# Four tiles of 320 tokens become tiles of 320, 448 and 512 in the first layer of an attention and two-layer feed-forward kernel

## The chip, the cores and the metric

The kernel runs on one core of one Trainium2 chip. The metric is device time in microseconds (us) of one execution, as the median of several runs. Beside it stands one profiled execution, from which all rows below come. Engines are named as in the profile: PE (TensorE matmuls), PEld (its weight loads), DVE (VectorE), ACT (ScalarE), POOL (GpSimd), SP (SyncE, which issues the transfers).

## The reference

Windowed attention with a linear distance bias, then two feed-forward layers, on 4 sequences of 576 tokens, 8 heads of 64:

```python
scores = scale * np.matmul(q, k.transpose(0, 1, 3, 2))
bias = slopes[:, None, None] * (-np.abs(rel).astype(np.float32))[None, :, :]
mask = (rel >= 0) & (rel < window)                   # window = 128
attn = softmax(np.where(mask, scores + bias[None], -1e9))
x = np.matmul(attn, v)                               # 2304 tokens x 512
h = x @ w_in;  x = (h * np.clip(h + 3.0, 0.0, 6.0) / 6.0) @ w_out      # layer 1, 512 -> 2048 -> 512
r = np.maximum(x @ w_in2, 0.0);  out = (s * r * r + b) @ w_out2        # layer 2, same sizes
```

Everything is float32.

## The kernel before, in words

**Layer 1.** A matrix product in float32 is made of three products of parts: each operand is split into a rounded high part and the rest. The 2304 tokens go through layer 1 in tiles. A tile takes 16 steps `f`, one for each 128 of the 2048 inner columns. Step `h` is 12 matmuls (4 blocks of 128 inputs, three products of parts) into one bank of PSUM; then ACT (`relu`) and DVE (`product`) make the gated value, ACT (`hi`) and DVE (`lo`) split it; step `o` is 12 matmuls into four banks that stay for the tile. Every matmul has 128x128 weights, and as many columns as the tile has tokens. Tiles 0 and 1 (256 tokens each) share their matmuls from step 4 on, 512 columns wide. Tiles 2 and 3 have 256 tokens; their `o` step covers two products with one matmul and takes 8. Tiles 4 to 7 have 320 tokens, the last 320 of each of the four sequences. `end` scales the four banks and stores them to `x2d` in DRAM.

**Attention.** A `Unit` is one head of one group of tokens, and units go in pairs of heads, 16 pairs for the four groups of 320. On PE a pair of that kind makes: scores `q` (line 606 here, 8 matmuls on quarters of the array, 64x64), one score matmul `hs` for the last half block (line 626), transposes `t` of the softmax weights (line 703: two for one head and three for the other) and the values product `v` (line 747, 8 matmuls on halves of the array, 128x64). Between them DVE takes row minima, ACT exponentials, POOL the division and the masks. Scores, transposes and values each take one of three banks (`tag="a", bufs=3`). The tokens of tile `t` have their attention while tile `t - 1` runs.

**Weights of layer 2.** Layer 2 uses sums and differences of blocks of its weights. A `Pair` loads 1 MB of the raw weights (two transfers, `load`), rebuilds floats from the given words (`high`, `rest` on ACT, `shift`, `sign` on DVE, `add` on POOL), forms differences (`sums`, DVE), splits them (`hi` on ACT, `lo` on DVE and POOL) and stores them to DRAM (`wh`, `wo`), from where layer 2 streams them. There are 16 pairs, all made during layer 1. They load into two buffers by turns and compute in a third (`work`).

**Order.** The program is a table written out by hand: each operation has a slot and a rank in it, `at(slot, rank, fn)`, and a table `MOVED` shifts single ones. Each engine works its list strictly in this order. A step `h` stands every second slot; step `o(f)` stands two steps after `h(f)`, so that PE alternates `o` and `h`. Attention pieces stand in the gap behind an `h`. While any tile but the last runs, `h` has a single bank (`tag="h"`), so `h(f + 1)` waits until `product(f)` has read it.

```python
starts = [74 + LATER, 97] + [first + 10 * i for i in range(2 * NP - EARLY)]     # slots at which pairs begin
self.raw = rawbuf[self.i % 2 if self.i >= EARLY else 0]                         # Pair.load
self.work = work() if self.i >= EARLY else rawbuf[1].bitcast(F32)
```

## Time and profile before

| | |
|---|---|
| median of 3 runs | 870.03 us (869.93 to 870.09) |
| profiled execution | 869.65 us, its span 867.9 us |
| PE busy | 860.3 us (99%), 5735 instructions |
| DVE, ACT, POOL busy | 615.7 (71%), 515.9 (59%), 347.9 us (40%) |
| transfers | 183.07 MB, mean 211 GB/s |

The span runs from the first to the last instruction; the profiled execution's time has 1.75 us more around it. Since matmuls are pipelined, the time of a matmul is read from the start of one row to the start of the next, not from its duration.

### The profile page before, as it was taken

How to read it: one execution, taken by the hardware profiler on the slowest of the kernel's cores; microseconds unless marked ns; L12 is line 12 of the kernel's file. 1: busy time of each engine (PE TensorE's matmuls, PEld its weight loads, DVE VectorE, ACT ScalarE, POOL GpSimd, SP SyncE). 2: the span in 40 equal slices, each digit the busy share in tenths (PEclk: the TensorE clock that was granted, in tenths of full speed). 3: DMA queues.
4: the chain of work that ended last, by engine and by line, in shares of the span. 5: the costliest groups of instructions: out<-in, count | busy, mean ns of one | idle time of the engine just before them, and what ended most of it. 6: DMA issues, size and time to landing. Idle time of an engine off the chain costs nothing.

```text
span 867.9 us, 16152 instructions
## 1 busy us (share of the span) xinstructions
PE 860.3 (99%) x5735; PEld 791.1 (91%) x5737; DVE 615.7 (71%) x1368; ACT 515.9 (59%) x1165; POOL 347.9 (40%) x549
## 2 busy tenths in 40 slices
PE   8999999999999999999999999999999999999998
PEld 5997778898989999999999999998899988999887
DVE  6869984577877666767656536779857789577784
ACT  7868985566666555656545436665256655366551
POOL 5647651345554544454444303462114450144200
PEclk9999999999999999999999999999999999999999
DMA  9526443536566555556463628787888887777873
GB/s 330 181 69 193 153 147 107 174 119 215 188 206 212 171 169 193 180 182 227 143 202 121 255 79 297 257 318 243 268 281 294 291 278 256 261 254 266 296 244 114
DMA packets 66879, 183.07 MB, mean 211 GB/s; under 512 B 9968, under 2 KB 29680, under 8 KB 58352
## 3 DMA queue, kind: packets, MB, share of 16 engines
q1 hardware_dynamic: 66800, 182.06, 62.3%
q8 instruction: 45, 0.74, 0.4%
q14 instruction: 34, 0.28, 0.1%
HBM read 143.13 MB, written 38.80 MB: 210 GB/s over the span
## 4 chain that ended last, share of the span: by engine, by line
PE 96%; ACT 1%; DVE 1%; issue 1%; DMA 1%; POOL 0%; SPq 0%; ACTq 0%
PE h L1004 23%; PE o L1052 23%; PE h L1547 20%; PE o L1481 20%; PE v L747 2%; PE s L606 1%; PE t L869 1%; PE tv L884 1%; PE t L703 1%; PE s L838 1%; PE s L591 1%; PE v L948 1%; PE s L626 1%; ACT P L860 0%; DMA raw<-qkv0p 0%
## 5 line engine op out<-in xcount | busy, mean ns | idle before, releaser
L1052 PE MATMUL o<-g,w 128*128 128x320 f32 (+2 forms) x1264 | 228.4, 328 | 0.2 <-DVE g L1029 0.2
L1052 PEld LDWEIGHTS o<-g,w 128*128 128x128 f32 x1264 | 192.3, 188 | 16.8 <-issue 6.2
L1004 PE MATMUL h<-both,w 128*128 128x320 f32 (+2 forms) x1200 | 197.7, 313 | 0.4 <-DVE t L1018 0.4
L1004 PEld LDWEIGHTS h<-both,w 128*128 128x128 f32 x1200 | 178.5, 188 | 7.7 <-DVE t L1018 0.9
L1018 DVE SCALAR_TENSOR_TENSOR t<-t,h 128x320 f32<-128x320 f32 (+2 forms) x116 | 56.0, 483 | 104.2 <-ACT t L1015 104.1
L1015 ACT ACTIVATE t<-h 128x320 f32<-128x320 f32 (+2 forms) x116 | 50.4, 435 | 130.6 <-PE h L1004 130.3
L1547 PE MATMUL h<-x,wstream 128*128 128x384 f32 x612 | 115.4, 335 | 0.0
L1547 PEld LDWEIGHTS h<-x,wstream 128*128 128x128 f32 x612 | 106.4, 188 | 0.8 <-ACT s L1557 0.6
L1481 PE MATMUL o<-wstream,i 128*128 128x512 f32 (+1 forms) x588 | 104.2, 333 | 0.0
L1481 PEld LDWEIGHTS o<-wstream,i 128*128 128x128 f32 x588 | 89.1, 188 | 11.3
L1581 ACT ACTIVATE g<-g,scalar 128x384 f32<-128x384 f32 x96 | 58.6, 610 | 39.4 <-DVE g L1566 37.0
L1481 PE MATMUL o<-both,i 128*128 128x256 f32 (+1 forms) x444 | 78.2, 332 | 0.0
L1547 PE MATMUL h<-x,both 128*128 128x384 f32 x396 | 76.4, 334 | 0.0
L1481 PEld LDWEIGHTS o<-both,i 128*128 128x128 f32 x444 | 66.6, 188 | 8.6
L1025 ACT ACTIVATE g<-t 128x320 fp32r<-128x320 f32 (+2 forms) x116 | 54.1, 466 | 28.4 <-DVE t L1018 27.8
L1029 DVE TENSOR_TENSOR g<-t,g 128x320 fp32r<-128x320 f32 (+2 forms) x116 | 61.9, 534 | 12.6 <-ACT g L1025 11.0
L1604 POOL TENSOR_TENSOR g<-g 128x384 f32<-128x384 f32 x24 | 24.3, 1014 | 112.4 <-PE h L1547 95.8
L1547 PEld LDWEIGHTS h<-x,both 128*128 128x128 f32 x396 | 69.3, 188 | 0.0
L1565 DVE TENSOR_TENSOR g<-h,s 128x384 f32<-128x384 f32 x72 | 39.8, 553 | 31.2 <-PE h L1547 22.5
L732 POOL TENSOR_SCALAR_AFFINE_SELECT W<-F 128x128 f32<-128x128 f32 (+1 forms) x128 | 38.0, 334 | 43.2 <-ACT F L707 41.2
L1221 POOL TENSOR_TENSOR work<-raw 128x512 int32<-128x512 int32 x28 | 29.9, 1086 | 50.3 <-DVE raw L1212 12.5
L1331 DVE SCALAR_TENSOR_TENSOR i<-g,scalar,i 128x768 fp32r<-128x768 f32 x48 | 49.2, 1072 | 0.6 <-ACT i L1330 0.6
(161 smaller groups left out, 1391.2 us busy)
## 6 DMA issues: line engine op xcount, KB each, us to landing
raw<-w SPq DMA_DIRECT2D x53, 512.0 KB, 5.5
wstream<-wo SPq DMA_DIRECT2D x24, 1024.0 KB, 4.9
both<-wo SPq DMA_DIRECT2D x18, 1024.0 KB, 5.9
wstream<-wh SPq DMA_DIRECT2D x18, 768.0 KB, 6.0
wstream<-wh SPq DMA_DIRECT2D x12, 1024.0 KB, 5.7
both<-wh SPq DMA_DIRECT2D x12, 1024.0 KB, 5.2
wh<-raw SPq DMA_DIRECT2D x16, 512.0 KB, 3.0
wo<-raw SPq DMA_DIRECT2D x16, 512.0 KB, 3.2
```

The costliest lines, as they stand in the source:

```text
L732: nc.gpsimd.affine_select(out=u.W[:, o : o + r], in_=self.F[:, q : q + r], fill=0.0, base=k - 1, compare_op=ALU.is_ge, pattern=[[s, r]], c ...
L1004: nc.tensor.matmul(self.ps, lhsT=w[:, wp, cc * P : (cc + 1) * P], rhs=self.values(cc, xp), start=m == 0, stop=m == 3 * CC - 1,)
L1015: nc.scalar.activation(self.a, self.ps, AF.Relu, bias=3.0)
L1018: nc.vector.scalar_tensor_tensor(out=self.a, in0=self.a, scalar=6.0, in1=self.ps, op0=ALU.min, op1=ALU.mult)
L1025: nc.scalar.activation(self.g[:, 0], self.a, AF.Copy)
L1029: nc.vector.tensor_tensor(out=self.g[:, 1], in0=self.a, in1=hi, op=ALU.subtract)
L1052: nc.tensor.matmul(self.sums()[d][:, : n * self.n], lhsT=w[:, wp, DM + d * P : DM + (d + 1) * P], rhs=self.g[:, gp : gp + n], start=f == 0 ...
L1331: nc.vector.scalar_tensor_tensor(out=out[:, :, 1], in0=src, scalar=b, in1=hi.bitcast(F32), op0=ALU.add, op1=ALU.subtract,)
L1481: nc.tensor.matmul(self.acc[k][c][:, out], lhsT=g[:, gp, c * P : (c + 1) * P], rhs=w[:, cols], start=k in (0, 1, 5) and p == 0 and i == 0, ...
L1547: nc.tensor.matmul(self.ps[first], lhsT=w[:, wp, cc], rhs=x[:, cc, xp], start=n == first and m == 0, stop=m == 5, skip_group_check=True,)
L1565: nc.vector.tensor_tensor(out=g, in0=self.ps[n], in1=self.s[j], op=ALU.add)
L1581: nc.scalar.activation(g, g, AF.Copy, scale=s_sb)
```

## The change

The last 1280 tokens are cut into five groups instead of four: the third sequence's last 320 tokens become groups of 128 and 192. Three tiles replace four: 320, 320 + 128 and 192 + 320 tokens. The units of the last four groups are of a new class, `LateUnit`, whose pairs begin every 4 slots, where pairs began every 8, and which goes from scores to values in 10 slots, where it was 16. The inputs `x` of all tiles lie in one stretch `both`; those of the 512-wide tiles begin 8 numbers (32 bytes) later in it than the others. A `Pair` now has two buffers in all: one for the raw weights, into which the high parts are written, and one for the sums, in which the rests are left in place; high and low parts are stored by a transfer each. Its stages take 9 slots in the first seven pairs and 4 in the others; the pairs begin at other slots, the last five in the last tile with a fresh raw buffer for each of the last four. `end` takes the four banks one by one. The table `MOVED` gets entries for the new class and some others.

```diff
-    groups = [(b, qa, qb) for qa, qb in ((0, 2), (2, NB)) for b in range(B)]
+    groups = [(b, 0, 2) for b in range(B)]
+    groups += [(0, 2, NB), (1, 2, NB), (2, 2, 3), (2, 3, NB), (3, 2, NB)]
+    TILES = ((0,), (1,), (2,), (3,), (4,), (5, 6), (7, 8))
...
+    XPLACES = (0, 0, 22, 0, 20, 0, 14)
+    both = xpool.tile([P, 30 * N1A + 16], F32R, name="both")
+    AHEAD = 8
...
+            x = both[:, XPLACES[t] * N1A + (AHEAD if t < 2 or n == 512 else 0) :][:, : 2 * CC * n]
...
+    class LateUnit(Unit):
+        def plan(self, s):
...
+                at(s + 1, 20.5, self.scores)
...
+                    at(s + 2, 20.7, self.half_scores)
...
+            at(s + 2, 32 + odd / 2, self.minima)
+            at(s + 3, 33 + odd / 2, self.exps)
+            at(s + 5 + odd, 31, self.weights)
+            k = s + odd
+            at(k + 7, 20, self.transposes)
...
+                at(s + 11, 20, self.values)
...
         def plan(self, s, load):
             self.s = s
+            k = lambda i: s + ((0, 0, 1, 2, 4, 4, 6, 7, 7, 8), (0, 0, 0, 1, 1, 2, 2, 2, 3, 3))[s >= NARROW][i]
...
         def load(self):
-            self.raw = rawbuf[self.i % 2 if self.i >= EARLY else 0]
-            self.work = work() if self.i >= EARLY else rawbuf[1].bitcast(F32)
+            i = self.i - FRESH
+            if i < 0:
+                self.raw = rawbuf[0]
+            else:
+                self.raw = wtile(i, [P, 4 * DM], I32, f"raw_{self.i}")
+            self.work = rawbuf[1 if i < 0 else i % 2].bitcast(F32)
...
-            nc.sync.dma_start(out=dst, in_=out)
+            nc.sync.dma_start(out=dst[:, :, :HB], in_=hi)
+            nc.sync.dma_start(out=dst[:, :, HB:], in_=lo)
...
-    starts = [74 + LATER, 97] + [first + 10 * i for i in range(2 * NP - EARLY)]
+    NARROW = hslot[5, 0]
+    starts = [80, 96, 110, 124, 138, 152, 165]
+    starts += [NARROW + 4 + 7 * i for i in range(4)] + [last + i for i in (1, 7, 12, 17, 22)]
+    FRESH = 12
...
-            Pair(i, i % NP, i // NP).plan(s, s - 5)
+            Pair(i, i % NP, i // NP).plan(s, s - (4 if s < NARROW else 3))
...
+            if u.g < 5:
+                u.plan(hslot[u.g, 0] - 20 - 4 * (H - 1 - u.h))
+            else:
+                t, i = (5, 2 * (u.h // 2) + (u.g == 5)) if u.g < 7 else (6, 2 * (u.h // 2) + (u.g == 8))
+                u.plan(hslot[t, 0] - 46 + 4 * i)
```

**On PE, in the first tile of 320** (step 4 of it). In the names, `v_2_3` are the values of heads 2 and 3, `s_2_6` the scores of head 6, `P` the softmax weights, `W` their masked transposes, the last number a buffer's. Before, the values product `v` of one pair of heads (the last two of its eight rows are shown) and the scores `q` of a later pair stand in one gap, directly behind each other, ahead of step `o`.

```order
L747 MATMUL v_2_3_3586<-W_2_2_3472,rv_2_2_3215 64x64
L747 MATMUL v_2_3_3586<-W_2_3_3525,rv_2_2_3215 64x64
L606 MATMUL s_2_6_3595<-raw_2_6_3340 64x192
L606 MATMUL s_2_7_3596<-raw_2_6_3340 64x192
L606 MATMUL s_2_6_3595<-raw_2_6_3340 64x192
L606 MATMUL s_2_7_3596<-raw_2_6_3340 64x192
L606 MATMUL s_2_6_3595<-raw_2_6_3340 64x192
L606 MATMUL s_2_7_3596<-raw_2_6_3340 64x192
L606 MATMUL s_2_6_3595<-raw_2_6_3340 64x192
L606 MATMUL s_2_7_3596<-raw_2_6_3340 64x192
L1052 MATMUL o_0_3436<-g_3_3566,w_3_633 128x320
```

In the new program the same tile has, in the gap behind step 3, three transposes and the scores of a pair:

```order
L1129 MATMUL h_3_3583<-both,w_3_634 128x320 x12
L796 MATMUL t_2_3_3596<-ident,P_2_3_3393 128x128 x2
L796 MATMUL t_2_3_3596<-ident,P_2_2_3388 128x128
L698 MATMUL s_2_4_3612<-raw_2_4_3398 64x192
L698 MATMUL s_2_5_3613<-raw_2_4_3398 64x192
L698 MATMUL s_2_4_3612<-raw_2_4_3398 64x192
L698 MATMUL s_2_5_3613<-raw_2_4_3398 64x192
L698 MATMUL s_2_4_3612<-raw_2_4_3398 64x192
L698 MATMUL s_2_5_3613<-raw_2_4_3398 64x192
L698 MATMUL s_2_4_3612<-raw_2_4_3398 64x192
L698 MATMUL s_2_5_3613<-raw_2_4_3398 64x192
L1177 MATMUL o_0_3513<-g_1_3543,w_1_366 128x320
```

The values of the pair before it stand a gap later, behind `h` of step 4, with `hs` ahead of them and a transpose behind them. So what stood in one gap is now in two. From the second tile of 256 on, before has 18 stretches of matmuls on parts of the array in such gaps (14 of `v` with `q` of this kind, 2 of the earlier kind of `v` with `q`, 2 of `v` alone); the new program has 38 (4 with both, 16 of `q` alone, 18 of `v` alone). Of the 18, 13 are followed by a transpose or by `hs`, which take the whole array. Between `h0_13` and `h0_14` in the shared part of tiles 0 and 1, two stretches that stood apart now stand together.

**On SP**, in the second tile of 320 of the old program and in the tile of 448 of the new one. Before, the load of a pair's raw weights goes to the buffer that the pair two earlier used, and the stores come from three buffers.

```order
L1191 DMA raw_202<-w 128x1024 x2
L568 DMA rv_2_4_4353<-v 128x512
L1282 DMA wo<-raw_201 128x2x512 x2
L1282 DMA wo<-staging_early 128x2x512
L1282 DMA wo<-work 128x512
```

Now all transfers of two pairs that follow each other use the same two buffers (202 raw, 203 sums), and the load stands directly behind the stores:

```order
L1398 DMA wo<-raw_202 128x2x256
L1399 DMA wo<-raw_203 128x2x256
L1398 DMA wo<-raw_202 128x2x256
L1399 DMA wo<-raw_203 128x2x256
L1398 DMA wo<-raw_203 128x256
L1399 DMA wo<-raw_203 128x256
L1398 DMA wo<-raw_202 128x2x256
L1399 DMA wo<-raw_203 128x2x256
L1313 DMA raw_202<-w 128x1024 x2
L660 DMA rv_3_6_5168<-v 128x2x192
```

A load that went out ahead of the stores of the pair before it now goes out behind them.

## Rows read from the trace of the kernel before

**Rows 1.** The page, part 4: chain that ended last, by engine.

```profile
PE 96%; ACT 1%; DVE 1%; issue 1%; DMA 1%; POOL 0%; SPq 0%; ACTq 0%
```

**Rows 2.** Waits of PE: total us, times, longest.

```profile
PE h L1004 <- DVE t L1018: 0.4, 2, 0.3
PE o L1052 <- DVE g L1029: 0.2, 1, 0.2
```

**Rows 3.** Windows: stretch, us, busy PE, PEld, DVE, ACT, POOL; clock; DMA.

```profile
252.00:446.00 194.00, 194.00 (x1513) 185.22 (x1512) 133.62 (x379) 116.20 (x303) 93.34 (x211) 1.00 0.55 181
```

**Rows 4.** Timeline of PE, tile 5 (320): start, us, line, matmuls.

```profile
354.10 1.92 PE L1052 MATMUL o<-g,w 128*128 128x320 f32 x12
355.86 1.92 PE L1004 MATMUL h<-both,w 128*128 128x320 f32 x12
357.71 1.31 PE L747 MATMUL v<-W,rv 128*64 128x128 f32 x16
358.95 0.88 PE L606 MATMUL s<-raw 64*64 64x192 f32 x16
359.76 2.03 PE L1052 MATMUL o<-g,w 128*128 128x320 f32 x12
361.62 1.93 PE L1004 MATMUL h<-both,w 128*128 128x320 f32 x12
```

**Rows 5.** Timeline of PE, tile 6: values with no scores behind them.

```profile
440.73 1.92 PE L1004 MATMUL h<-both,w 128*128 128x320 f32 x12
442.58 1.31 PE L747 MATMUL v<-W,rv 128*64 128x128 f32 x16
443.82 2.02 PE L1052 MATMUL o<-g,w 128*128 128x320 f32 x12
445.68 1.92 PE L1004 MATMUL h<-both,w 128*128 128x320 f32 x12
```

**Rows 6.** Timeline of PE: 512 columns wide, tiles 0 and 1.

```profile
131.64 3.05 PE L1004 MATMUL h<-both,w 128*128 128x512 f32 x12
134.53 0.49 PE L869 MATMUL t<-ident,P 128*128 128x128 f32 x3
134.77 2.99 PE L1052 MATMUL o<-g,w 128*128 128x512 f32 x12
137.61 1.58 PE L1004 MATMUL h<-x,w 128*128 128x256 f32 x12
139.03 2.91 PE L1052 MATMUL o<-g,w 128*128 128x512 f32 x12
141.86 0.87 PE L948 MATMUL v<-W,rv 128*64 128x256 f32 x8
142.66 0.93 PE L591 MATMUL s<-raw 64*128 64x128 f32 x8
```

**Rows 7.** Groups by line and form, 250 to 440 us: a pair's operations (mean ns).

```profile
L1200 ACT ACTIVATE work<-raw 128x1024 f32<-128x1024 f32 x9 | 10.3, 1140 | 0.5 <-DVE staging_early L1273 0.3 <-ACT both L758 0.2
L1203 ACT ACTIVATE raw<-raw 128x1024 int32<-128x1024 uint32 x9 | 10.3, 1149 | 0.0
L1212 DVE SCALAR_TENSOR_TENSOR raw<-raw,work 128x1024 int32<-128x1024 int32 x9 | 11.0, 1222 | 0.1
L1221 POOL TENSOR_TENSOR work<-raw 128x512 int32<-128x512 int32 x18 | 19.2, 1086 | 34.1 <-DVE raw L1212 11.2 <-ACT P L665 6.5 <-ACT F L707 5.9
L1248 DVE TENSOR_TENSOR work<-work 128x256 f32<-128x256 f32 x36 | 15.7, 463 | 1.9 <-POOL work L1221 0.9
L1268 ACT ACTIVATE raw<-work 128x512 fp32r<-128x512 f32 x18 | 10.3, 623 | 0.0
L1273 POOL TENSOR_TENSOR raw<-work,raw 128x256 fp32r<-128x256 f32 x19 | 14.9, 805 | 8.4 <-ACT raw L1268 8.4
```

**Rows 8.** DMA issues: KB each, median us from issue to landing.

```profile
raw<-w SPq DMA_DIRECT2D x53, 512.0 KB, 5.5
wh<-raw SPq DMA_DIRECT2D x16, 512.0 KB, 3.0
```

More of the change, by code (lines that the diff above doesn't have):

```diff
@@ L63 @@
     "Ha0.lo": (-1, 1.7),
-    "Ha0.load": (1, 0),
+    "Ha0.sign": (0, -3.8),
     "Ha1.hi": (0, 2.1),
@@ L84 @@
     "M1.fold": (-1, 4.14),
-    "M1.masks": (-1, 0),
+    "M1.masks": (1, 1.43),
+    "M1.minima": (0, 2.2),
     "M1.values": (-1, 0),
-    "M1.weights": (2, 7),
-    "P0.load": (-1, 0),
+    "M1.weights": (2, -2),
+    "P0.add": (0, 6),
+    "P0.rest": (0, 9.8),
+    "P1.rest": (0, 1.8),
     "S00.copy": (1, 0),
@@ L112 @@
     "T320.relu": (0, 0.15),
+    "Tl.h": (-1, -1),
     "U0.minima": (-1, 6),
     "U0.scale": (1, 6.0),
+    "U1.transposes": (0, 3),
+    "U1.values": (-1, -1),
     "U1.weights": (2, 0),
+    "V50.fold": (-1, 1.15),
+    "V50.load": (-1, 0),
+    "V50.lower": (0, -0.65),
+    "V50.scale": (0, 8.5),
+    "V51.exps": (1, 0),
+    "V51.masks": (-1, 2.13),
+    "V60.exps": (-1, 0),
+    "V60.load": (-2, 0),
+    "V60.masks": (-1, 4.98),
+    "V60.minima": (-1, 1.0),
+    "V61.exps": (1, 0),
+    "V61.minima": (1, 0.8),
+    "V61.values": (0, -9.5),
+    "V70.fold": (-1, 9.7),
+    "V70.load": (-1, 0),
+    "V70.lower": (0, -1.5),
+    "V70.minima": (-1, 0),
+    "V70.scale": (0, 2.8),
+    "V71.fold": (-1, 1.7),
+    "V80.exps": (-1, 0),
+    "V80.fold": (-1, 0),
+    "V80.load": (-1, 0),
+    "V80.lower": (-1, 4.9),
+    "V80.scale": (0, -0.46),
+    "V80.weights": (0, -0.92),
+    "V81.weights": (-1, -0.8),
     "H0_1.hi": (-1, 0),
@@ L177 @@
     "T2_7.o": (1, 0),
+    "T4_1.o": (1, 12),
+    "T5_1.h": (0, 12),
+    "T5_1.relu": (-1, 1.95),
+    "T5_3.o": (0, 10),
+    "T6_14.h": (-1, 0.5),
+    "T6_15.o": (-1, 10.3),
+    "T6_7.relu": (-1, 0),
+    "T6_8.hi": (-1, 8.95),
+    "U0.half_exps": (-1, 0),
+    "U0.half_minima": (-1, 0),
     "U0.half_weights": (0, -1.4),
-    "U0.load_values": (3, 0),
+    "U0.load_values": (5, 35.5),
+    "U0_2_2.load": (1, 0),
     "U0_2_3.values": (0, 0.8),
+    "U1.to_lo": (1, -0.6),
+    "V1_2_0.fold": (0, 1.3),
+    "V1_2_7.weights": (0, 0.6),
+    "V2_2_0.exps": (1, 0),
+    "V2_2_2.scores": (0, 0.5),
+    "V2_2_3.weights": (1, -0.4),
+    "V2_2_7.lower": (-1, 0),
+    "V2_3_2.transposes": (-1, 0.8),
+    "V2_3_5.exps": (0, -1.35),
+    "V50.half_exps": (0, 4.1),
+    "V50.half_weights": (1, -1.6),
+    "V50.load_values": (-1, 32.3),
+    "V51.to_hi": (0, -0.2),
+    "V60.load_values": (-1, 0),
+    "V70.load_values": (3, 29.4),
+    "V71.to_hi": (0, -0.36),
+    "V80.half_exps": (0, -0.06),
+    "V80.half_weights": (1, 4.5),
+    "V81.to_hi": (-1, 7.6),
+    "V81.to_lo": (1, -1.3),
 }
@@ L1064, in end @@
         def end(self):
-            for e in range(0, CC, 2):
-                ys, stores = self.places(e)
+            n = self.n
+            for d, a in enumerate(self.sums()):
+                y = self.place(d)
                 if self.wide:
-                    for y, a in zip(ys, self.sums()[e : e + 2]):
-                        nc.scalar.activation(y, a[:, self.n :], AF.Copy, scale=1.0 / 6.0)
-                        nc.vector.scalar_tensor_tensor(
-                            out=y, in0=a[:, : self.n], scalar=1.0 / 6.0, in1=y,
-                            op0=ALU.mult, op1=ALU.add,
-                        )
+                    nc.scalar.activation(y, a[:, n:], AF.Copy, scale=1.0 / 6.0)
+                    nc.vector.scalar_tensor_tensor(
+                        out=y, in0=a[:, :n], scalar=1.0 / 6.0, in1=y, op0=ALU.mult, op1=ALU.add
+                    )
+                elif d % 2 == 0:
+                    nc.scalar.activation(y, a, AF.Copy, scale=1.0 / 6.0)
@@ new lines, in end, with groups, place @@
+                c = 0
+                for g in self.groups():
+                    nc.sync.dma_start(out=x2d[g][:, d], in_=y[:, c : c + SIZES1[g]])
+                    c += SIZES1[g]
+        def groups(self):
+            return TILES[self.t]
+        def place(self, d):
+            n = self.n
+            if self.t == nt1 - 1:
+                if d in (1, 2):
+                    return gpool.tile([P, 512], F32, tag="t", name=f"y{self.t}_{d}")[:, :n]
+            elif d and d * n <= 2 * DM:
+                return late["early"][:, (d - 1) * n : d * n]
+            elif self.t == 0 and d == 3:
+                return rawbuf[1].bitcast(F32)[:, :n]
+            elif self.t == 5 and d == 3:
+                return gpool.tile([P, 512], F32, tag="t", name=f"y{self.t}_{d}")[:, :n]
+            return gpool.tile([P, 512], F32, tag="y", bufs=1, name=f"y{self.t}_{d}")[:, :n]
```

233 lines of the change are left out of this document (118 added, 115 removed).

## The prediction

> **What bounds it now.** I read the chain of work that ended last first: 96% of it is PE [rows 1]. Then the waits of PE: the steps of layer 1 wait 0.6 us for DVE, in three places [rows 2]. Then the windows: between 252 and 446 us, where the tiles of 320 run with attention in their gaps, PE is busy for 194.00 of 194.00 us at a granted clock of 1.00, which is the 2.4 GHz level, while DVE is busy 69%, ACT 60% and POOL 48% of it [rows 3]. The reader is to see that no other engine sets the pace: the time is the sum of what PE has in its list, start to start. So I price the change on PE first, and ask then what could make PE wait. The timeline gives the prices, from the start of one row to the start of the next.
>
> **Prices on PE.** A step without attention behind or ahead of it: `o` at 354.10, `h` at 355.86, so 1.76 us for 12 matmuls, 146.7 ns for 320 columns [rows 4]. The `h` that a `v` follows takes 1.85 us, so going over to a part of the array costs 0.09 us. `v` takes 1.24 us, `q` 0.81 us. The `o` behind `q` takes 1.86 us, so coming back costs 0.10 us [rows 4]. `v` alone: again 1.85, then 1.24, then 1.86 us [rows 5]. So `v` with `q` is 0.09 + 1.24 + 0.81 + 0.10 = 2.24 us, `v` alone 1.43 us, and `q` alone, which no row shows, 1.00 us by the same borders. What was 2.24 us together is 2.43 us apart: each stretch more costs 0.19 us.
>
> The Trainium skill's page TensorEngine Tiling (Array Packing), Key Properties, says of this that changing the tiling mode drains the engine, and gives no price. It speaks against a change that makes more such changes of mode; the trace agrees with it at the 0.09 and 0.10 us above.
>
> For 512 columns: `o` from 139.03 to 141.86, less the 0.09 us for the `v` behind it, is 2.74 us, 228 ns a matmul. `h` from 131.64 to 134.53 takes 2.89 us where `o` in the same surroundings, 134.77 to 137.61, takes 2.84: 4 ns more a matmul, so 232 ns [rows 6]. 448 columns no row shows; on the line between 320 and 512 it is 201 ns in `o` and 204 ns in `h`.
>
> **The change, part by part.**
>
> *Tiles.* Four tiles of 320 have 4 x 16 x 24 = 1536 matmuls: 1536 x 146.7 ns = 225.3 us. Now there are 384 less: the tile of 320 takes 56.3 us, that of 448 takes 192 x (201 + 204) ns = 77.8 us, that of 512 takes 192 x (228 + 232) ns = 88.3 us, in all 222.4 us: **2.9 us less**. If `o` at these widths went no faster than `h`, it would be 56.3 + 78.3 + 89.1 = 223.7 us, 1.6 us less; if time went with the columns alone, nothing. That is the small end.
>
> *Place of x.* The 512-wide inputs move by 32 bytes. Nothing in the trace says why `h` is 4 ns behind `o`; if the place is the cause, 144 matmuls of tiles 0 and 1 and 192 of the last tile gain up to 4 ns each, 1.3 us; if not, nothing. I take half, **0.6 us less**.
>
> *Attention.* From tile 2 on there are 38 stretches where there were 18. Twenty more at 0.19 us are 3.8 us. Eight of them come from cutting one group of 320 into two: its four `v` and four `q` go in two pieces each. A `v` of the earlier kind has 768 columns in its four matmuls and takes 0.80 us [rows 6]; this one has 1280 and takes 1.24 us: 0.14 us of it don't go with the columns. Eight pieces more at 0.14 us are 1.1 us; at the least, pieces in proportion, nothing. Thirteen stretches are followed by a transpose or an `hs` instead of `o`; what coming back costs there no row shows: between nothing and 0.10 us, I take 0.05, so 0.65 us less. The sum is 3.8 + 1.1 - 0.65 = **4.3 us more**, from 3.8 - 1.3 = 2.5 to 4.9. The transposes and `hs` are as many as before.
>
> *Two small ones.* Two stretches between `h0_13` and `h0_14` now touch: 0.19 us less. There is one change of tile less, worth at most the 0.2 us that `o` waited for DVE [rows 2]; I take 0.1. Together **0.3 us less**.
>
> *Work at no cost on PE.* The number of operations per token on DVE, ACT and POOL stays or falls with the wider tiles, and none is near full [rows 3]. Sixteen pairs of weights stay sixteen; doubled stores and smaller loads of q and k lie on SP's queue, beside PE. Their cover is PE's list; if one is late, a wait appears, next.
>
> *Waits.* The gaps are fuller: scores to values take 10 slots instead of 16, so results are wanted sooner from engines that queue strictly. Layer 1 of the kernel before has 0.6 us of PE waits [rows 2]. I add half of that again, **0.3 us**; nothing at the least, and the rival below at the most.
>
> **Sum.** -2.9 - 0.6 + 4.3 - 0.3 + 0.3 = +0.8 us on the profiled execution's 869.65 us: 870.45. The median of the runs shown is 0.38 us over that execution, so the forecast is **870.8 us**. A measurement of this kernel can tell about 0.2% (1.7 us) from no change: this is none.
>
> **Rivals.**
>
> *A wait for weights (slower).* In the tile of 448 a pair begins every 7 slots, and each uses the same two buffers, so its load can only go out when the stores before it have landed; the q, k and values of the next heads, which stand behind it on SP's queue, wait with it. In turn: load 5.5 us [rows 8], `high` 1.14, `rest` 1.15, `sign` 1.22, `add` 2 x 1.09, the differences 4 x 0.46, `hi` 0.62, `lo` on POOL 2 x 0.81, the store 3.0 us [rows 7, 8]: 18.3 us with no queueing. Seven slots are 3.5 pairs of steps of 12 x 405 ns = 4.86 us, 17.0 us, and with attention, two pairs of heads in four gaps, at least 3.5 x 1.1 us more: 20.9 us. There are 2.6 us for all queueing behind attention on ACT, DVE and POOL. If it takes more, `high` stands at the head of ACT's queue and waits for its load; behind it stands the `relu` of the next `h`, behind that `product` on DVE, and PE cannot write the next `h`, whose bank is single. Four pairs that each make PE wait 0.8 us give 3.2 us in place of the 0.3: +3.7 us, 873.7 us. For it: before, loads ran ahead of the stores into another buffer. Against it: PE's `o` step of 2.4 us covers a part of each delay, and the row of `high` shows ACT waiting 0.5 us in all for nine pairs [rows 7]. It decides from 2.6 us of queueing a pair on.
>
> *Wider matmuls give next to nothing (slower).* If time goes with the columns, the tiles save nothing, and the place of x neither: the sum is +0.8 + 2.9 + 0.6 = +4.3 us, 874.3 us. For it: `h` at 512 columns is 232 ns, 0.454 ns a column, against 0.458 at 320. Against it: `o` at 512 is 0.445. In the same direction goes the page TensorE: Matmul & The Clock Gate, Back-to-back issue gap, of the Trainium skill: a warm matmul takes N / 2.4 + 2.5 ns, so that 384 matmuls less at equal columns save an estimated 1.0 us, and the sum by it is +2.7 us, 872.7 us. The trace differs from it: 146.7 ns at 320 columns, where the page gives 135.8.
>
> *Cheap stretches (faster).* If coming back to a transpose costs nothing and pieces go in proportion, attention adds 2.5 us, and if the place of x gives all of its 1.3 us, with no new wait: -2.9 - 1.3 + 2.5 - 0.3 = -2.0 us, 868.0 us. Against it: all bounds must fall on one side.
>
> That the change doesn't do what it says is excluded by the order: three tiles, 384 matmuls less.
>
> **Chances.** The forecast 0.53 (its own range 869.5 to 871.7 us); the wait for weights, or another of the kind at the same price, 0.25; no gain from width 0.10; cheap stretches 0.12. Faster by over 0.2% (under 868.3 us) then has 0.12, within 0.2% 0.53, slower (over 871.8 us) 0.35. For 8 in 10 I go from 868.6 us, which leaves out most of the faster case, to 874.0 us, between the prices of the two slower ones.
>
> **What would show it.** In the timeline after: 12 matmuls of 448 columns in 2.41 to 2.45 us and of 512 in 2.74 to 2.79 us, `h` at 512 as fast as `o` if its place matters; `q` alone at 0.81 us, with 1.85 us for the `h` ahead and 1.86 us for the `o` behind at 320 columns; a PE busy share as before, and PE waits of about 1 us in layer 1. Waits of `h` on `product` (DVE) in the tile of 448, and idle time of ACT ahead of `high` ended by a transfer, would show the first rival. What would make the prediction wrong is a wait in a place that I have not looked at: the three banks of scores, transposes and values, which now pass round once in a gap, or the change to layer 2: its first weights are stored later, and its fourth and fifth load go out only when the last tile's x is free, two slots ahead of it. I cost that at nothing, since they are wanted after ten products or more; one that came too late would cost up to its landing time, 5.5 us for half a megabyte [rows 8].

## The result: 0.7% slower, outside the range

The changed kernel takes 876.77 us (median of 4 runs, 876.48 to 877.70), the kernel before in the same series 870.06 us. The ratio is 1.0071, with a 95% interval of 1.0049 to 1.0093: slower, and 6.0 us over the forecast. The profiled execution has a span of 875.0 us where it was 867.9: 7.1 us more.

The page of the changed kernel, first the busy time of each engine, then the chain that ended last (answering to [rows 1]):

```profile
span 875.0 us, 15673 instructions
PE 864.9 (99%) x5367; PEld 768.0 (88%) x5369; DVE 628.6 (72%) x1370; ACT 512.8 (59%) x1147; POOL 364.6 (42%) x565
...
PE 94%; ACT 2%; DMA 1%; DVE 1%; issue 1%; POOL 1%; SPq 0%; DVEq 0%; ACTq 0%
```

PE has 368 instructions less and is busy 4.6 us longer. It still sets the pace; its share of the chain falls from 96% to 94%, and ACT's rises from 1% to 2%. The waits of PE in layer 1, answering to [rows 2]; `t`, `s` and `tv` in other rows of this view belong to attention ahead of tile 2:

```profile
PE o L1177 <- DVE y L1195: 1.3, 1, 1.3
...
PE t L796 <- POOL raw L648: 0.4, 1, 0.4
PE h L1129 <- DVE t L1143: 0.3, 1, 0.3
PE o L1177 <- DVE g L1154: 0.2, 1, 0.2
```

Before, these tiles had 0.6 us of waits; one new wait alone takes 1.3 us. The windows (columns as in [rows 3]) say where PE stands still and where not. The first is of the kernel before; the other two are of the changed kernel, of most of layer 1 behind tile 1, and of the rest of its last tile with all of layer 2.

```profile
183.00:450.00 267.00, 266.81 (x2102) 251.08 (x2101) 188.38 (x549) 161.87 (x434) 131.78 (x298) 1.00 0.58 187
...
183.00:450.00 267.00, 265.11 (x1869) 233.11 (x1868) 181.38 (x545) 149.87 (x415) 130.32 (x299) 1.00 0.53 163
450.00:868.00 418.00, 418.00 (x2315) 384.90 (x2314) 308.13 (x444) 227.25 (x408) 141.49 (x120) 1.00 0.74 263
```

Between 183 and 450 us PE lacks 1.9 us of 267; before, it lacked 0.2. Behind 450 us it lacks nothing, at a granted clock of 1.00 (the 2.4 GHz level), so what is lost in layer 2 is lost inside the matmuls.

The timeline of the changed kernel, in order of time (SPq are SP's transfers at issue): a pair's load and the border from tile 2 to tile 3; attention in the tile of 320; steps of 448 columns; steps of 512.

```profile
189.41 0.37 SPq L1399 DMA_DIRECT2D wh<-raw  x1
189.88 1.90 SPq L1313 DMA_DIRECT2D raw<-w  x2
...
198.09 1.13 ACT L1322 ACTIVATE raw<-raw 128x1024 f32<-128x1024 f32 x1 [1.29 <-DMA raw<-qk]
...
199.31 0.69 DVE L1329 TENSOR_SCALAR raw<-raw 128x1024 int32<-128x1024 int32 x1 [2.06 <-ACT raw L1322]
...
202.48 0.42 DVE L1195 SCALAR_TENSOR_TENSOR y<-o,y 128x256 f32<-128x256 f32 x1
...
202.95 1.68 PE L1177 MATMUL o<-g,w 128*128 128x256 f32 x8 [1.30 <-DVE y L1195]
...
286.77 1.92 PE L1129 MATMUL h<-both,w 128*128 128x320 f32 x12
288.63 0.66 PE L842 MATMUL v<-W,rv 128*64 128x128 f32 x8
289.22 0.44 PE L796 MATMUL t<-ident,P 128*128 128x128 f32 x2
289.41 2.01 PE L1177 MATMUL o<-g,w 128*128 128x320 f32 x12
...
414.18 2.62 PE L1129 MATMUL h<-both,w 128*128 128x448 f32 x12
416.64 2.63 PE L1177 MATMUL o<-g,w 128*128 128x448 f32 x12
...
429.48 2.60 PE L1177 MATMUL o<-g,w 128*128 128x448 f32 x12
431.92 2.90 PE L1129 MATMUL h<-both,w 128*128 128x512 f32 x12
...
502.38 2.88 PE L1129 MATMUL h<-both,w 128*128 128x512 f32 x12
505.10 2.88 PE L1177 MATMUL o<-g,w 128*128 128x512 f32 x12
507.82 2.88 PE L1129 MATMUL h<-both,w 128*128 128x512 f32 x12
```

Start to start, `h` of 448 columns takes 2.46 us (414.18 us) and `o` 2.44 us (429.48 us), and both steps of 512 take 2.72 us, 227 ns a matmul: the tiles do what was forecast. Line L1322 is `high`, L1329 `shift`, L1195 the emptying of the four banks by `end`.

Summed from start to start over all rows of PE's timeline, with idle time taken out and put by itself, the 7.1 us are:

| part, us | forecast | measured |
|---|---|---|
| tiles and place of x, change of tile | -3.6 | -3.2 |
| attention | +4.1 | +5.2 |
| idle time of PE in layer 1 | +0.3 | +2.1 |
| layer 2 | 0 | +2.7 |
| behind the last matmul | 0 | +0.3 |
| sum | +0.8 | +7.1 |

The split between the first two rows depends on which duration is taken as a step's bare price, and holds to some 0.7 us; their sum, +2.0, doesn't depend on it.

### The profile page after: what moved, and what is told of

Its sections match the earlier page's. It is cut to its first block, busy times and chain, and to the rows that moved or that the text cites. A ratio compares the mean times of both kernels' runs of the same rounds, so it can differ in the third digit from the quotient of the medians.

```text
span 875.0 us, 15673 instructions
## 1 busy us (share of the span) xinstructions
PE 864.9 (99%) x5367; PEld 768.0 (88%) x5369; DVE 628.6 (72%) x1370; ACT 512.8 (59%) x1147; POOL 364.6 (42%) x565
## 4 chain that ended last, share of the span: by engine, by line
PE 94%; ACT 2%; DMA 1%; DVE 1%; issue 1%; POOL 1%; SPq 0%; DVEq 0%; ACTq 0%
PE o L1177 22%; PE h L1129 22%; PE o L1597 20%; PE h L1663 20%; PE v L842 2%; PE s L698 1%; PE t L796 1%; PE tv L1009 1%; PE t L994 1%; PE s L683 1%; PE v L1073 1%; DMA raw<-qkv0p 1%; PE s L719 1%; PE s L963 0%; DMA raw<-qk 0%
## 5 line engine op out<-in xcount | busy, mean ns | idle before, releaser
L1177 PE MATMUL o<-g,w 128*128 128x512 f32 (+3 forms) x1072 | 222.5, 355 | 1.6 <-DVE y L1195 1.3
L1129 PE MATMUL h<-both,w 128*128 128x256 f32 (+3 forms) x1200 | 218.6, 331 | 0.4 <-DVE t L1143 0.3
L1663 PE MATMUL h<-x,both 128*128 128x384 f32 x630 | 117.0, 337 | 0.0
L1597 PE MATMUL o<-both,i 128*128 128x512 f32 (+1 forms) x600 | 103.2, 332 | 0.0
L1140 ACT ACTIVATE t<-h 128x256 f32<-128x256 f32 (+3 forms) x100 | 47.6, 476 | 91.7 <-PE h L1129 90.1
L1143 DVE SCALAR_TENSOR_TENSOR t<-t,h 128x256 f32<-128x256 f32 (+3 forms) x100 | 53.6, 536 | 62.0 <-ACT t L1140 61.7
L1154 DVE TENSOR_TENSOR g<-t,g 128x256 fp32r<-128x256 f32 (+3 forms) x100 | 63.8, 638 | 20.9 <-ACT g L1150 18.9
L1150 ACT ACTIVATE g<-t 128x256 fp32r<-128x256 f32 (+3 forms) x100 | 50.9, 509 | 39.0 <-DVE t L1143 33.3
L1663 PE MATMUL h<-x,wstream 128*128 128x384 f32 x378 | 72.2, 337 | 0.0
L1389 POOL TENSOR_TENSOR raw<-raw,raw 128x256 fp32r<-128x256 f32 x60 | 51.9, 885 | 24.7 <-ACT raw L1384 24.7
```

The costliest lines, as they stand in the source:

```text
L1129: nc.tensor.matmul(self.ps, lhsT=w[:, wp, cc * P : (cc + 1) * P], rhs=self.values(cc, xp), start=m == 0, stop=m == 3 * CC - 1,)
L1140: nc.scalar.activation(self.a, self.ps, AF.Relu, bias=3.0)
L1143: nc.vector.scalar_tensor_tensor(out=self.a, in0=self.a, scalar=6.0, in1=self.ps, op0=ALU.min, op1=ALU.mult)
L1150: nc.scalar.activation(self.g[:, 0], self.a, AF.Copy)
L1154: nc.vector.tensor_tensor(out=self.g[:, 1], in0=self.a, in1=hi, op=ALU.subtract)
L1177: nc.tensor.matmul(self.sums()[d][:, : n * self.n], lhsT=w[:, wp, DM + d * P : DM + (d + 1) * P], rhs=self.g[:, gp : gp + n], start=f == 0 ...
```

## The experiments

Two theories stood for the two new losses. *Layer 2*: its matmuls are slower because the 64 bytes added to `both` and the shift of x put its operands at other places; the rival is that the change to its loads or stores does it. *Layer 1*: the loads of the raw weights come late, and the engines that work their lists in order pass the delay on to PE; the rival is that attention's faster sequence makes the waits by itself, so that a wait taken away comes back elsewhere. Differences of time below are against the kernel before in the same series, whose medians lay between 869.85 and 870.05 us.

**Places put back** (label e1_x_back, the changed kernel with x and the size of `both` as they were):

```diff
-    both = xpool.tile([P, 30 * N1A + 16], F32R, name="both")
+    both = xpool.tile([P, 30 * N1A], F32R, name="both")
-    AHEAD = 8
+    AHEAD = 0
```

> The changed kernel with the first layer's 512-wide inputs moved back by 32 bytes and the 64 bytes that they took at the end of their buffer given back, so that the second layer's streamed weights and its x lie 64 bytes lower, as in the kernel before. Theory A (place): the slower matmuls of layer 2 (512 columns 232.0 ns where they were 229.2, 256 columns 118.5 for 117.5, 384 columns 174.6 for 173.8, in all 2.7 us) come from these 64 bytes: they go back to 229, 117.5 and 173.8, and the first layer's h of 512 columns falls back from 227 to some 233 ns, 336 matmuls, 1.6 to 2.0 us; in all 0.7 to 1.1 us less than the changed kernel, about 875.9. Theory B (something else in the new weights or their transfers makes layer 2 slower): layer 2 stays at 232 ns and only the 1.6 to 2.0 us of h are added, 878.6.

Measured: 879.15 us (874.65 to 880.80), ratio 1.0096 (1.0065 to 1.0127); the profiled span is 872.9 us. Groups by line and form of layer 2's product (count, then busy us and mean ns of one) before:

```profile
L1481 PE MATMUL o<-both,i 128*128 128x512 f32 x204 | 71.5, 392 | 0.0
L1547 PE MATMUL h<-x,both 128*128 128x384 f32 x396 | 76.4, 334 | 0.0
```

in the changed kernel:

```profile
L1663 PE MATMUL h<-x,both 128*128 128x384 f32 x630 | 117.0, 337 | 0.0
L1597 PE MATMUL o<-both,i 128*128 128x512 f32 x264 | 93.6, 397 | 0.0
L1597 PE MATMUL o<-wstream,i 128*128 128x512 f32 x216 | 75.7, 391 | 0.0
```

and with the places put back:

```profile
L1663 PE MATMUL h<-x,both 128*128 128x384 f32 x630 | 116.8, 335 | 0.0
L1597 PE MATMUL o<-both,i 128*128 128x512 f32 x264 | 91.9, 392 | 0.0
```

In the changed kernel the row of 512 columns on `both` is 5 ns longer, the one on `wstream` is not; the row of 384 columns is 3 ns longer. With the old places the first is as before, and the second within 1 ns. Start to start over all of layer 2, the matmuls of 512, 256 and 384 columns take 229.2, 117.7 and 173.8 ns before, 232.0, 118.5 and 174.6 changed, and 229.2, 117.7 and 173.7 put back: with 480, 551 and 1008 of them that is 2.7 us, all of layer 2's loss. So it is a matter of place, and not of loads or stores, which are the same in both. `h` at 512 columns in layer 1 goes the other way, from 230.4 to 235.7 ns, 1.8 us for 336 matmuls. The median didn't fall with it; the waits differ from execution to execution, as the repeat of this kernel shows below.

The place that counts is not simply that of a matmul's own operands. The 64 bytes stand at the end of `both`, which begins at the same byte in both kernels, and its rows are counted from its start. So the streams that `o<-both` reads lie where they lay, and so does the other operand, `i`; yet these matmuls lose most, 5 ns. What moves is what lies behind `both`: two of the five streams (`wstream`), not all as I had expected, the tokens and layer 2's x.

**Which place?** Three kernels move things otherwise: label e2_streams_1600 makes `both` 64 bytes longer still, e4_tokens_back puts 496 numbers ahead of the tokens, and e9_all_32 shifts all of x and the streams alike.

```diff
-    both = xpool.tile([P, 30 * N1A + 16], F32R, name="both")
+    both = xpool.tile([P, 30 * N1A + 32], F32R, name="both")
```

> The changed kernel with 64 bytes more behind the inputs, so that the streamed weights and x of layer 2 lie 128 bytes further than before, and 64 further than in the changed kernel; the 32 bytes ahead of the first layer's inputs stay. Theory A, if what counts is the place modulo 128 bytes: layer 2 as before, 2.7 us less, 874.1. If any place but the old one is slower, or theory B: no change, 876.8. The h of 512 columns in layer 1 stays at 227 ns in each.

Measured: 878.44 us, ratio 1.0095 (1.0078 to 1.0111). The matmuls of 512 columns fall to 230.5 ns, those of 384 rise to 176.1; layer 2 as a whole gains nothing. By the rows, `o` on `both`, whose operands again haven't moved, is as fast as before, and `o` on `wstream` has become slower by 2 ns:

```profile
L1597 PE MATMUL o<-both,i 128*128 128x512 f32 x264 | 92.0, 392 | 0.0
L1597 PE MATMUL o<-wstream,i 128*128 128x512 f32 x216 | 76.2, 393 | 0.0
```

```diff
+        pool.tile([P, 496], F32, name="pad", tag="pad")
         late["xr"] = tiles(pool, 2, "xr", (2, TT))
```

> The changed kernel with 1984 bytes left free ahead of the second layer's x, so that x alone lies again as in the kernel before modulo 2048 bytes; the streamed weights stay 64 bytes further. Theory A, with x at cause for the h of layer 2 alone: the 384-column matmuls go from 174.6 back to 173.8 ns, 0.9 us less, 875.9, and the 512-column ones stay at 232. If the place of the two streams is at cause for all: no change, 876.8; if x is at cause for all: 874.1.

Measured: 877.31 us, ratio 1.0082 (1.0067 to 1.0097); 232.0 and 175.0 ns: nothing comes back. Since the tokens and x then lie as before modulo 2048 bytes, their place, as far as that is what counts, isn't what slows the matmuls of 512 columns; of what lies behind `both`, the two streams are left.

```diff
-    both = xpool.tile([P, 30 * N1A + 16], F32R, name="both")
+    both = xpool.tile([P, 30 * N1A + 8], F32R, name="both")
-            x = both[:, XPLACES[t] * N1A + (AHEAD if t < 2 or n == 512 else 0) :][:, : 2 * CC * n]
+            x = both[:, XPLACES[t] * N1A + AHEAD :][:, : 2 * CC * n]
-        return both[:, row * N1A :][:, : rows * N1A].bitcast(F32)
+        return both[:, row * N1A + AHEAD :][:, : rows * N1A].bitcast(F32)
```

> The changed kernel with all inputs of layer 1 and all streamed weights and x of layer 2 moved to 32 bytes past a multiple of 64, where the weights of layer 1 and the stationary operands of layer 2 lie (in the changed kernel only the 512-wide inputs of layer 1 lie so). Theory A2 (two operands at the same place modulo 64 bytes run fastest): the 512-column matmuls of layer 2 take 227 ns (232.0 in the changed kernel, 229.2 before), the 256-column ones 117 (118.5, 117.5), the 384-column ones at most 173.8 (174.6): 2.7 us and up to 1.2 us more less than the changed kernel, 873 to 874. Rival (only the old place, 1472 modulo 2048 bytes, runs at 229.2): 876.8 or more.

Measured: 876.60 us (874.03 to 879.27), ratio 1.0078 (1.0055 to 1.0100); 230.0, 117.2 and 173.7 ns. Of the 2.7 us 2.6 come back, and the waits of layer 1 take most of them again (PE idle between 183 and 450 us 3.7 us, for 1.9). So places matter, but no single rule of place fits all these kernels: which of them slow which matmuls, and how the place of a stream can slow a matmul that doesn't read it, stays open.

**The kernel before with x moved by 32 bytes** (label e10_before_32):

```diff
-    first_two = both[:, : 4 * CC * N1A].rearrange("p (c h n) -> p c h n", c=CC, h=2)
+    first_two = both[:, 8 : 8 + 4 * CC * N1A].rearrange("p (c h n) -> p c h n", c=CC, h=2)
```

> The kernel before with one change: the 512-wide inputs of tiles 0 and 1 begin 32 bytes further in their buffer, all else lies where it lay. In the changed kernel the h of 512 columns went from 233 to 227 ns a matmul with this. If the place does it alone: 144 matmuls by 5 to 6 ns, 0.7 to 0.9 us less than before, 869.2, with layer 2 unchanged at 229.2, 117.7 and 173.7 ns. If the faster h belonged to something else in the change: 870.0.

Measured: 869.90 us (12 runs), the kernel before 869.87 (17 runs), ratio 0.9999 (0.9989 to 1.0008). `h` at 512 columns falls from 239.6 to 237.0 ns, some 0.4 us for 144 matmuls. Here nothing moves but x, which these matmuls read. The gain of place is real in the rows and too small here for the time.

**Values a gap later, in the kernel before** (label e6_values_apart): 14 stretches of `v` with `q` become two each, nothing else.

```diff
+    "U1.values": (1, 0),
```

> The kernel before with one change: the values product of each pair of heads from the first unit of the tiles of 320 on stands one gap later, beside the transposes of the next pair, in place of beside the scores. In 14 places a stretch of v with q becomes two, one of q and one of v and t. By the prediction a stretch more costs 0.19 us, less 0.05 in front of a transpose: 14 times 0.14, 2.0 us more than before, 872.1. If a transpose behind v saves nothing: 14 times 0.19, 2.7 us more, 872.7. If stretches cost nothing beside a transpose: 870.1.

Measured: 881.88 us, ratio 1.0141 (1.0124 to 1.0158), the largest loss of a single line here. The timeline of PE:

```profile
347.44 1.92 PE L1005 MATMUL h<-both,w 128*128 128x320 f32 x12
349.28 0.88 PE L607 MATMUL s<-raw 64*64 64x192 f32 x16
350.09 2.03 PE L1053 MATMUL o<-g,w 128*128 128x320 f32 x12
351.96 1.92 PE L1005 MATMUL h<-both,w 128*128 128x320 f32 x12
353.81 1.31 PE L748 MATMUL v<-W,rv 128*64 128x128 f32 x16
355.05 0.44 PE L704 MATMUL t<-ident,P 128*128 128x128 f32 x2
355.25 2.00 PE L1053 MATMUL o<-g,w 128*128 128x320 f32 x12
357.08 1.92 PE L1005 MATMUL h<-both,w 128*128 128x320 f32 x12
```

`q` alone adds 1.84 + 0.81 + 1.87 - 2 x 1.76 = 1.00 us, as forecast. `v` with two transposes behind it adds 1.85 + 1.24 + 0.20 + 1.83 - 2 x 1.76 = 1.60 us. Joined they were 2.24 us, and the two transposes alone 0.22 us (16 times before): a stretch more costs 1.00 + 1.60 - 2.46 = 0.14 us where nothing waits, 2.0 us for 14. The span is 11.7 us longer. The rest is waiting and what stands behind it: PE is idle 6.3 us between 183 and 462 us where it was 0.2, ahead of that 0.8 us more, and the rows on both sides of a wait are longer: around the 0.30 us wait of the `h` at 285.80 us, `o` and `h` take 0.27 us more than the same two rows from 355.25 us on. The waits of PE:

```profile
PE o L1053 <- DVE y L1071: 3.0, 2, 1.5
...
PE h L1005 <- DVE t L1019: 1.7, 5, 0.5
...
PE o L1053 <- ACT g L1026: 1.1, 2, 0.6
```

A stretch is cheap; values that come a gap later were not in this kernel, whose order was made for the earlier place. The waits name DVE and ACT; that they come from what hangs on the values, now in these engines' lists beside the work of tiles and weights, fits them and isn't shown apart. One of these waits, 1.48 us, stands at the border from tile 2 to tile 3, where ACT waits for no load (it has landed at 198.90 us, and `high` begins at 203.61): denser lists alone can make as long a wait there as the changed kernel has.

**The 1.3 us at the border.** In the timeline above, the load of pair 3 goes out at 189.88 us, behind the store at 189.41, since one buffer holds the raw weights of all pairs up to the twelfth. Its two transfers take 6.2 us from issue to landing (median); before, the same two took 6.4, so they are not slower. ACT stands at `high` for 1.29 us; DVE stands at `shift` for 2.06 us, behind it in DVE's list is the emptying of tile 2's banks, and `o` of tile 3 waits 1.30 us for that. Before, the load of this pair went out at 191.17 us and `high` began at 201.63: 10.5 us, none of them idle. So the load goes out no later than it did; `high` is wanted earlier, at 196.80 us. If this chain is the cause, PE's wait has to follow ACT's idle time one for one. Two kernels change only what goes out on SP beside this load. Label e16_load_alone lets q and k of one pair of heads go three slots later:

```diff
+    "U0_2_6.load": (3, 0),
```

> The changed kernel with one move: the six loads of q and k that stand on SP's queue right behind the load of the third pair of weights (0.38 MB beside its 1 MB) go out behind the stores of tile 2 instead, so that the pair's load has the transfer engines nearly to itself; no work on PE, DVE or ACT is moved, on POOL only the clearing of that buffer. Theory C (the late landing of this load is what PE waits for at the border): ACT's idle time ahead of the third pair falls from 1.3 us to under 0.4, PE's wait with it, one for one, and with it 0.3 us of starting again: about 1.2 us less than the changed kernel, 875.5, if the q and k come in time. Rival D (the border is full whatever the load does): 876.8 or more, with the wait as it was.

Measured: 876.00 us (875.65 to 877.67), ratio 1.0077 (1.0062 to 1.0092). The timeline of ACT and PE:

```profile
197.43 1.16 ACT L1323 ACTIVATE raw<-raw 128x1024 f32<-128x1024 f32 x1 [0.61 <-DMA raw<-w]
...
202.31 1.68 PE L1178 MATMUL o<-g,w 128*128 128x256 f32 x8 [0.68 <-DVE y L1196]
```

Label e17_load_behind puts the load one place later on SP:

```diff
-        Pair(i, i % NP, i // NP).plan(s, s - (4 if s < NARROW else 3))
+        Pair(i, i % NP, i // NP).plan(s, s - (0 if i == 2 else 4 if s < NARROW else 3))
```

> The other way round, the same load one place later on SP's queue, behind the load of values (256 KB) that stood behind it, all else as in the changed kernel. Theory C: ACT's idle time and PE's wait at the border grow together by the 0.5 us that a place on the queue takes and by the share of the 256 KB that now goes first, 0.5 to 1.5 us more, 877.3 to 878.3. Rival D: 876.8.

Measured: 877.32 us, ratio 1.0087 (1.0070 to 1.0104). The same two engines:

```profile
198.51 1.15 ACT L1322 ACTIVATE raw<-raw 128x1024 f32<-128x1024 f32 x1 [1.90 <-DMA raw<-w]
...
201.67 0.41 PE L796 MATMUL t<-ident,P 128*128 128x128 f32 x2 [0.47 <-DVE st L741]
203.38 1.20 PE L1177 MATMUL o<-g,w 128*128 128x256 f32 x4 [1.30 <-DVE y L1195]
```

ACT idle 0.61 us, PE waits 0.68; 1.29 and 1.30 in the changed kernel; 1.90 and 0.47 + 1.30. In the thirteen profiles that have this chain, the changed kernel's among them, the two differ by 0.15 us at most. That this load, late for `high`, makes this wait is shown.

**The same kernel again** (label e15_x_back_again, the edit of e1_x_back):

> The kernel with the inputs moved back by 32 bytes once more, for the profile of another execution, since its four executions lay between 874.65 and 880.80 us. Theory C: an execution that takes longer shows more idle time of ACT ahead of the pairs of weights (3.2 us ahead of the seventh pair and under 0.2 us ahead of the others in the one profiled), and PE waits behind it; layer 2's matmuls stay at 229.2, 117.7 and 173.7 ns. Rival: the difference lies in layer 2 or at the end.

Measured: 876.75 us (877.25, 876.24), the profiled span 875.5 us where the first had 872.9. Layer 2 is the same to 0.1 ns. In the first profile ACT waited 0.11 us at `high` of pair 3 and PE 0.19 us at the border, in the second 1.06 and 1.10 us; at 253 us PE waited 0.50 us where it hadn't, behind a load for which ACT waited 2.15 us, for nothing in the first. So one kernel's loads take up to 1.5 us more in one run than in another (the load ahead of 253 us 5.6 and 7.2 us), and where a load has no time to spare this can reach the total. It is one reason why medians of four here differ by 2 us; that it is the only one isn't shown.

**Moving what stands behind the load.** Label e3_sign_behind puts `sign` of this pair behind the emptying of the banks:

```diff
+    "P2.sign": (1, -6.6),
+    "P2.add": (0, 1),
```

> The changed kernel with the 1.22 us sign operation of the third pair of weights put behind the evictions of tile 2 and the next product on DVE, and the additions on POOL that need it a rank later. Theory: the wait of the first o of tile 3 for DVE (1.3 us) goes with what PE lost in starting again (0.2 to 0.3 us): 1.3 to 1.6 us less, 875.3. Rival: the pair is late then, and a later product or store waits as long: 876.8.

Measured: 877.09 us, ratio 1.0078 (1.0063 to 1.0093). The wait at the border is 0.17 us, and PE waits 0.43 and 0.53 us 4 and 8 us later: given back.

Label e8_load_later takes a different load out of the way, ahead of the 0.4 us wait of a transpose at 244 us (which the profile puts down to the zeroes that POOL writes beside q):

```diff
+    "V1_2_2.load": (1, 0),
```

> The changed kernel with one load of q and k, that of the second pair of heads of the cut group's neighbour, one slot later, so that POOL's clearing of its buffer no longer stands ahead of POOL's scaling of the probabilities that the next transpose waits for. Theory: the transpose at 244 us waits no more: 0.4 us of wait and some 0.3 us behind it go, 0.7 us less, 876.1. Rival: it waits for the same scaling on POOL anyway, 876.8.

Measured: 877.99 us, ratio 1.0095 (1.0076 to 1.0113), that wait unchanged at 0.42 us. The load was not what it hung on; what it does hang on stays open.

**Giving the load time.** Label e11_load_early plans pair 2 two slots earlier, and the load of pair 3 too:

```diff
-    starts = [80, 96, 110, 124, 138, 152, 165]
+    starts = [80, 94, 110, 124, 138, 152, 165]
-        Pair(i, i % NP, i // NP).plan(s, s - (4 if s < NARROW else 3))
+        Pair(i, i % NP, i // NP).plan(s, s - (6 if i == 2 else 4 if s < NARROW else 3))
```

> The changed kernel with the second pair of weights begun two slots earlier, so that its buffer is free two slots earlier and the load of the third pair goes out 3.4 us earlier; the work on the third pair stays where it was. Theory C (a late load is all that makes PE wait at the border of tiles 2 and 3): ACT sits idle under 0.3 us ahead of the third pair, PE's wait of 1.3 us shrinks to 0.3 us or less and 0.3 us of starting again goes with it, 1.3 us less, 875.4. Rival D (DVE and ACT are full there whatever the load does, or the second pair now makes PE wait in tile 2): 876.8 or more.

Measured: 878.05 us, ratio 1.0098 (1.0080 to 1.0116). The load went out at 192.8 us, not earlier: it still waits for the stores of pair 2, whose own load was late now (ACT idle 1.63 us, PE 0.70 us at 173 us). At the border 0.66 us of ACT and 0.72 of PE. With e9_all_32's places (label e12_both):

> The earlier load of the third pair together with the move of all inputs and streams to 32 bytes past a multiple of 64. If the two causes are independent, the 2.1 us of layer 2 and the 1.3 us of the wait both go: 873.3 where the changed kernel takes 876.8. If a late load of the seventh pair still makes the scores at 324 us wait by 1 us, as it did when only the places were moved: 874.3. What then stays over the kernel before is attention in more stretches.

Measured: 876.86 us, ratio 1.0083 (1.0062 to 1.0103), ACT 1.45 and PE 1.30 us.

Label e7_pairs_later moves pairs 3 to 5 a slot later, with loads a slot further ahead:

```diff
-    starts = [80, 96, 110, 124, 138, 152, 165]
+    starts = [80, 96, 111, 125, 139, 152, 165]
-        Pair(i, i % NP, i // NP).plan(s, s - (4 if s < NARROW else 3))
+        Pair(i, i % NP, i // NP).plan(s, s - (5 if i in (2, 3, 4) else 4 if s < NARROW else 3))
```

> The changed kernel with the work on the third, fourth and fifth pair of weights begun one slot later while their loads go out where they did. Theory C (the loads come too late): ACT, which sat idle 1.3 us ahead of the third pair and 1.1 us ahead of the fifth for their transfers, waits no more there, DVE's evictions of tile 2 stand ahead of the pair's work, and PE's wait of 1.3 us at the first o of tile 3 goes, with 0.3 us of starting again and 0.3 us at 255 us: 1.6 to 1.9 us less, 875.0. Rival D (DVE and ACT are full at the border of tiles whatever the loads do): the wait is given back within the next steps, as it was when the sign operation alone stood behind, 876.8.

Measured: 881.36 us, ratio 1.0133 (1.0118 to 1.0148). ACT doesn't wait for these loads any more, and the wait at the border falls from 1.30 to 0.12 us; but PE has larger waits elsewhere:

```profile
PE s L698 <- DVE both L857: 1.7, 2, 1.4
PE h L1129 <- DVE t L1143: 1.4, 2, 1.1
```

Label e13_short_chain shortens a pair's stages from 9 to 7 slots, so that stores are out earlier, and loads accordingly:

```diff
-            k = lambda i: s + ((0, 0, 1, 2, 4, 4, 6, 7, 7, 8), (0, 0, 0, 1, 1, 2, 2, 2, 3, 3))[s >= NARROW][i]
+            k = lambda i: s + ((0, 0, 1, 2, 3, 3, 4, 5, 5, 6), (0, 0, 0, 1, 1, 2, 2, 2, 3, 3))[s >= NARROW][i]
-        Pair(i, i % NP, i // NP).plan(s, s - (4 if s < NARROW else 3))
+        Pair(i, i % NP, i // NP).plan(s, s - ((4, 4, 7, 7, 7, 7, 6)[i] if s < NARROW else 3))
```

> The changed kernel with the work on each of the first seven pairs of weights drawn together from eight slots to six, and the loads of the third to the seventh pair sent out two or three slots earlier, since the stores before them are out earlier. Theory C (late loads): the loads have 3.5 to 5.4 us more, ACT waits under 0.3 us ahead of each pair, PE's wait at the border of tiles 2 and 3 (1.3 us and 0.3 us of starting again) and the 0.3 us at 255 us go: 1.6 to 1.9 us less than the changed kernel, 875.0, and executions lie closer together. Rival D (the engines have no room for the pair's work in fewer slots): new waits for DVE, ACT or POOL in tiles 2 to 4, 877 or more.

Measured: 884.12 us, ratio 1.0158 (1.0133 to 1.0182). ACT idle is nothing for pairs 4 to 8, and PE waits 2.1 us for `s` at 233 us and 2.4 us for the emptying of banks. Half of the latter is the old wait, for at pair 3 the load is still late (ACT idle 1.16 us, PE 1.20); the other half and the 2.1 us are new:

```profile
PE o L1177 <- DVE y L1195: 2.4, 2, 1.2
PE s L698 <- DVE both L857: 2.1, 1, 2.1
```

With e9_all_32's places (label e14_short_32):

> The shorter chains and earlier loads together with the move of all inputs and streams to 32 bytes past a multiple of 64, which took 2.1 us from the matmuls of layer 2. If both causes are as I think: 872.9, and no execution over 875. If the engines have no room: 875 or more.

Measured: 883.49 us, ratio 1.0159 (1.0139 to 1.0180). The matmuls of layer 2 are as fast as in e9_all_32 (230.0 ns at 512 columns); the waits of layer 1 are as in e13_short_chain, or longer.

So both theories on layer 1 hold, each for its part: the late load makes the 1.3 us wait at the border, and where it is given time, new waits for DVE come up elsewhere. The 0.4 us at 244 us have no cause shown. A second buffer for the raw weights, which would take the wait away without moving work, wasn't tried: no room was left for it. Nor were `q` and `v` joined again in the new class, which needs more than the three banks that they share. None of the kernels here beats the one before.

## Why the prediction was wrong

The bound and the prices of the tiles were right. Three terms were not: attention was sized too small, the waits in layer 1 were worked out for the wrong tiles, and layer 2 was put at nothing.

**Right.** PE is still the bound. 448 columns take 205 and 203 ns (forecast 204 and 201), 512 columns 227 ns, and `h` is as fast as `o` there: the place of x was the cause of the 4 ns. By the rows of e1_x_back it gives 1.8 us, over the 1.3 us that I had as the most. `q` alone costs 1.00 us, as priced. The rival by which width gives next to nothing has fallen. The Trainium skill's page TensorE: Matmul & The Clock Gate, Back-to-back issue gap, gives an estimated 215.8 ns at 512 columns. The trace has 227.

**Attention: +4.1 forecast, +5.2 measured; mis-sized.** Where nothing waits, the rows add up to 4.8 us. A stretch more costs 0.14 us beside a transpose, inside the forecast's 0.14 to 0.19. The pieces cost more: values in pieces take 0.59 us for 8 matmuls (above) and 0.81 us for 12, four times each, where the whole of 16 took 1.24 [rows 4], and scores 0.49 us for half of what took 0.81, eight times: 0.6 + 0.7 = 1.3 us in all, where I had 1.1; one stretch of values with `hs` behind it took 0.2 us more than its parts. Some 0.4 us are rows beside a wait. What is left, 0.3 us, is inside the 0.7 us of the split and has no row of its own.

**Waits: +0.3 forecast, +2.1 measured.** Here a step failed. The first rival, a wait for weights, happened, but not in the tile of 448, where ACT doesn't wait for any load. I worked out its slack only there, where pairs begin every 7 slots, and not for the tiles of 256 and 320, where they begin every 13 or 14. But there the stages are spread over 9 slots: the last store of pair 2 goes out 17.7 us after its `high` at 171.74 us, the next load has landed 8.6 us behind that, at 197.99 us, and `high` is wanted 25.1 us after the one before, at 196.80 us. The load is 1.2 us late. At pair 4 it has landed 1.2 us early (223.66 us, for `high` at 224.87), and nothing waits. The groups by line show it for `high` in the changed kernel (idle time of ACT ahead of it, us and times), against 0.5 us for nine pairs before, none of it ended by a transfer [rows 7]:

```profile
  DMA wo<-raw: 6.2, 1
  DMA raw<-qk: 4.1, 4
  DMA raw<-w: 0.9, 1
```

The 4.1 and 0.9 us are pairs 3 and 5 to 8; of these PE shows a wait behind pair 3 alone, the 1.3 us. The rest of the 2.1 us, 0.4 us at 244 us and some 0.5 us ahead of 183 us, has no cause shown. The 6.2 us stand in the last tile, at 452 us, and cost PE nothing. The form was also another: I expected `h` to wait for `product`; it was `o` at a border, because the emptying of four banks stands in DVE's list behind `shift`.

**Layer 2: 0 forecast, +2.7 measured.** The step "I cost that at nothing" failed by another mechanism than those that I named. The loads of layer 2 are in time, and PE waits for none; the 64 bytes that made room for the shift in layer 1 slowed the matmuls of layer 2, half of it in those of 512 columns on `both`. I had the difference of 4 ns in the rows [rows 6] and no reason for it, and asked only where it could help. No run here shows what lies behind the 3 to 5 ns; they come and go with the 64 bytes, also where a matmul's own operands haven't moved. The Trainium skill's page SBUF — State Buffer, section SBUF: two separate sides, says that PE never waits on anyone at the engines' ports of that memory; no run here shows whether that holds in these rows.

**The 0.2 us saved** between `h0_13` and `h0_14` can't be seen in the sum; PE's gaps ahead of 183 us grew by 0.5 us.

## What to carry to other kernels

When stores and the next load share one buffer, work out the beat for every stage of the program, not only the tightest: time from first use to last store, plus landing, against the distance of two uses; where less than 2 us are left, landing times that differ by 1.5 us from run to run can be a wait at whatever stands behind it in an engine's list. A buffer made longer moves all that lies behind it: compare the time of every matmul after it, not only of those that read what moved. And where PE is full, moving attention costs more than the changes of mode (0.14 us each, 2.0 us in e6_values_apart): results that come a gap later took most of the other 9.7 us there, in an order that wasn't made for them.
